# Linear attention with decay ahead of a soft mixture of experts: half of the heads with chunks of 64 tokens, scores made one chunk ahead

## The chip, the core and the metric

The kernel runs on one core of a Trainium2 chip. Five engines work side by side, each through its own list of instructions in order: TensorE (PE, with its weight loads shown apart as PEld), VectorE (DVE), ScalarE (ACT), GpSimd (POOL) and SyncE (SP), which here issues nearly all transfers. The measure is the time of one execution on the device in microseconds (us); lower is better. All data are f32.

## What is computed

The reference, cut to what matters:

```python
# B, H, S, D = 4, 8, 768, 64; block = 64
for b in range(nb):
    qb, kb, vb = q[:, :, sl], k[:, :, sl], v[:, :, sl]
    intra = einsum('bhic,bhjc->bhij', qb, kb) * Dmask      # lam**(i-j) for i >= j
    intra = einsum('bhij,bhjd->bhid', intra, vb)
    inter = einsum('bhid,bhde->bhie', qb * lam_pow, kv_state)
    out[:, :, sl] = intra + inter
    kb_dec = kb * rev_pow
    kv_state = lam_block * kv_state + einsum('bhsd,bhse->bhde', kb_dec, vb)
x = out.transpose(0, 2, 1, 3).reshape(B * S, H * D)        # 3072 x 512
logits = x @ phi                                           # 32 slots, 8 experts
d = softmax(logits, axis=0); slot_input = d.T @ x
h = relu(slot_input[e] @ w1[e]); slot_out[e] = h @ w2[e]   # for each expert e
return softmax(logits, axis=1) @ slot_out
```

The result of the attention doesn't depend on how long a block is: what lies inside a block goes through masked scores, what lies before it through the carried state.

## The kernel before

The tokens are cut into chunks of 128, 6 for each of 4 sequences, 24 in all (`T`, `NB = 6`). A head pair lies on the 128 partitions: `hh` is the half (partitions 0 to 63 or 64 to 127), `hp` one of the 4 pairs. The loop over `t` does, for every chunk:

- `scores(t)`: PE makes key times query for 8 heads into two banks (`sc`), in pieces of 64 keys, so that four instructions fill the four 64 x 64 quarters of the array. DVE multiplies them by the mask of powers of lam into `at`.
- `recall(t)`: queries decayed by POOL (`qs`, made by `decay_q`) times the state of the chunks before (`st`), into the banks `xa` and `xb`.
- `turn_k(t + 1)`: PE turns the keys of the next chunk through the bank `kv`, ACT copies them out (`kn`). For the chunks named by `loaded` a second copy of the keys, already turned, is loaded from memory instead (`kN`, 9 chunks).
- `natural(t - 1)`: PE turns the result of the last chunk (`tr`), ACT copies it to `x`.
- `attend(t)`: values times `at`, added to `xa` and `xb`; ACT copies them to `xt`.
- `state(t)`: decayed keys (`kd`, POOL) times values into `kv`; DVE adds it to the decayed state, giving `st`; POOL decays that into `dec` for the next chunk.

Every four chunks the soft mixture gets its part: in the chunk with t % 4 == 0 `logits` (bank `gl`, DVE reduction `mx`, ACT exponential `e`, DVE copy `L`), in the next one `weights` (two transposes in the bank `dp`), the first half of `slot_softmax` and `slots` (bank `gl`, DVE sum `acc`), in the third the rest of `slot_softmax` (`cs`, `CN`). After the loop come the last chunk's logits, the two layers of the experts (`first`, `second`; weights w1 in 32 slabs of 512 KB, w2) and the output (`put`: PE, a copy by ACT or DVE to `o`, a write of 256 KB `y<-o` by SP).

The order on every engine is that of the program: the class `InOrder` records each operation as it is written, so its line (L51 before, L49 after) stands for nearly all instructions, and a reader goes by the names of tiles. SP issues in program order too and waits where a buffer isn't free yet. `NLOAD` buffers take queries, keys and values; `NSLAB` slabs take weights, of which `PACE` tenths are asked for per chunk:

```python
if t + 2 < T:
    load_chunk(t + 2, (0, 1))
want = min(NSLAB, (t + 1) * PACE // 10)
load_early(want - sent)
```

PSUM, into which PE writes, has 8 banks, and all are named: sc0, sc1, xa, xb, kv, tr, gl, dp.

Of the kernel before, what the change touches and what calls it, by code (L numbers as in the profile page):

```python
# [14 lines left out]
P = 128  # L15
B, H, S, DH = 4, 8, 768, 64
# [8 lines left out]
NSLAB = 35  # L25
NLOAD = 10
# [6 lines left out]
PACE = 16  # L33


def loaded(t):

    return t == 0 or t % NB in (2, 4)
# [18 lines left out]
def decay_attn_soft_moe(  # L57
# [32 lines left out]
    def load_chunk(t, which=(0, 1, 2, 3)):  # L90
        srcs = (qT, kT, vN, kN)
        for i in which:
            if i == 3 and not loaded(t):
                continue
            tl = loads.tile([P, 512], F32, tag="ld", name="ld")
            sp.dma_start(out=tl, in_=srcs[i][t])
            IN[t, i] = tl
# [38 lines left out]
    load_chunk(0)  # L136
    load_chunk(1)
# [12 lines left out]
    wps = bank("dp")  # L150
# [15 lines left out]
    mask = work.tile([P, 2, HP, P], F32, tag="mask", name="mask")  # L166
    for hh in range(2):
        for hp in range(HP):
            x = hh * HP + hp
            dve.tensor_tensor_scan(  # L170
                out=mask[:, hh, hp, :],
                data0=lam_sb[:, x:x + 1].broadcast_to([P, P]),
                data1=ident,
                initial=0.0,
                op0=ALU.mult,
                op1=ALU.add,
            )
# [15 lines left out]
    kpow = mask.rearrange("p a b i -> p (a b) i")[:, :, P - 1:P]  # L193
# [8 lines left out]
    AT, XT, X, ST, QS, KD = {}, {}, {}, {}, {}, {}  # L202

    SC = {}

    def scores(t):
        q_, k_ = IN[t, 0], IN[t, 1]
        banks = [bank(f"sc{hh}") for hh in range(2)]

        for hp in range(HP):  # L210
            for j in range(2):
                for hh in range(2):
                    r = slice(64 * hh, 64 * hh + 64)
                    pe.matmul(
                        out=banks[hh][64 * j:64 * j + 64, hp * P:(hp + 1) * P],
                        lhsT=k_[r, hp * P + 64 * j:hp * P + 64 * j + 64],
                        rhs=q_[r, hp * P:(hp + 1) * P],
                        start=True,
                        stop=True,
                    )  # L220
        AT[t] = []
        for hh in range(2):
            at = work.tile([P, HP, P], F32, tag="at", name="at", bufs=2)
            sc = banks[hh].rearrange("p (a b) -> p a b", a=HP)
            dve.tensor_tensor(out=at, in0=sc, in1=mask[:, hh], op=ALU.mult)
            AT[t].append(at)

    def decay_q(t):
        if t < T and t % NB > 0:
            qs = work.tile([P, HP, P], F32, tag="qs", name="qs")  # L230
            pool.tensor_tensor(out=qs, in0=IN[t, 0].rearrange("p (a b) -> p a b", a=HP), in1=qpow, op=ALU.mult)
            QS[t] = qs

    def turn_k(t):

        if t < T and t % NB < NB - 1 and not loaded(t):
            tk = bank("kv")
            for hp in range(HP):
                pe.transpose(tk[:, hp * P:(hp + 1) * P], IN[t, 1][:, hp * P:(hp + 1) * P], ident)
            kn = work.tile([P, D], F32, tag="kn", name="kn")  # L240
            act.copy(out=kn, in_=tk)
            IN[t, 3] = kn

    def decay_k(t):
        if t < T and t % NB < NB - 1:
            kd = work.tile([P, H, DH], F32, tag="kd", name="kd")
            k_ = IN[t, 3]
            pool.tensor_tensor(
                out=kd.rearrange("p (a b) c -> p a b c", a=2),
                in0=k_.rearrange("p (a b c) -> p a b c" if loaded(t) else "p (b a c) -> p a b c", a=2, b=HP),  # L250
                in1=kpow.rearrange("p (a b) o -> p a b o", a=2).broadcast_to([P, 2, HP, DH]),
                op=ALU.mult,
            )
            KD[t] = kd

    XB = {}

    def place(t, hh, hp):

        g, a = divmod(hp, 2)  # L260
        return XB[t][hh][64 * a:64 * a + 64, g * P:(g + 1) * P]

    def recall(t):
        XB[t] = [bank("xa"), bank("xb")]
        if t % NB > 0:

            qs, st = QS.pop(t), ST["st"]
            for hp in range(HP):
                for hh in range(2):
                    r = slice(64 * hh, 64 * hh + 64)  # L270
                    pe.matmul(
                        out=place(t, hh, hp),
                        lhsT=st[r, hp, :],
                        rhs=qs[r, hp, :],
                        start=(hp < 2),
                        stop=True,
                        skip_group_check=True,
                    )

    def attend(t):  # L280
        n = t % NB
        v_ = IN[t, 2].rearrange("p (h c) -> p h c", h=H)
        at = AT.pop(t)
        xt = keep.tile([P, HP, P], F32, tag="xt", name="xt")
        for hh in range(2):
            for hp in range(HP):
# [3 lines left out]
                    rhs=at[hh][:, hp, :],  # L290
                    start=(n == 0 and hp < 2),
                    stop=True,
                    skip_group_check=True,
                )
            act.copy(
# [3 lines left out]

    def state(t):  # L300
        n = t % NB
        if n == NB - 1:
            return
        v_ = IN[t, 2].rearrange("p (h c) -> p h c", h=H)
        kd = KD.pop(t)
        kv = bank("kv")
        for hp in range(HP):
            for hh in range(2):
                pe.matmul(
                    out=kv[64 * hh:64 * hh + 64, hp * DH:(hp + 1) * DH],  # L310
                    lhsT=kd[:, HP * hh + hp, :],
                    rhs=v_[:, HP * hh + hp, :],
                    start=True,
                    stop=True,
                )
        kvv = kv[:, 0:HP * DH].rearrange("p (a b) -> p a b", a=HP)
        st = work.tile([P, HP, DH], F32, tag="st", name="st", bufs=2)
        if n == 0:
            dve.tensor_copy(out=st, in_=kvv)
        else:  # L320
            dve.tensor_tensor(out=st, in0=ST["dec"], in1=kvv, op=ALU.add)
        ST["st"] = st
        if n < NB - 2:
            dec = work.tile([P, HP, DH], F32, tag="dec", name="dec")
            pool.tensor_tensor(
                out=dec, in0=st, in1=lamc.broadcast_to([P, HP, DH]), op=ALU.mult
            )
            ST["dec"] = dec
# [12 lines left out]
    def logits(g):  # L341
        cs = [t for t in range(4 * g, 4 * g + 4) if t < T - 1]
        R = SL * len(cs)
        pl = bank("gl")
        for hp in range(HP):
            for c, t in enumerate(cs):
# [6 lines left out]
                )  # L353
        pl = pl[0:R, 0:P]
# [29 lines left out]
    def weights(raw=True):  # L384
        dp = bank("dp")
# [3 lines left out]
        dve.tensor_copy(out=d, in_=dp[:, 0:P])  # L389
        return dp[:, P:2 * P]  # L390

    def slot_softmax(g, lp):

        lv = lp.rearrange("p (g s) -> p g s", g=4)
# [20 lines left out]
    def slots(g):  # L415
        cs = [t for t in range(4 * g, 4 * g + 4) if t < T - 1]
        R = SL * len(cs)
        psl = bank("gl")
        for c, t in enumerate(cs):
# [6 lines left out]
            )  # L426
        if g == 0:
# [13 lines left out]
    sm = iter(())  # L441
    for t in range(T):
        if t + 2 < T:
            load_chunk(t + 2, (0, 1))

        want = min(NSLAB, (t + 1) * PACE // 10)
        load_early(want - sent)
        sent = max(sent, want)
        if t + 2 < T:
            load_chunk(t + 2, (2, 3))  # L450
# [3 lines left out]
        for _ in range((2, 4, 3)[t - T + 3] if t >= T - 3 else 0):  # L454
            load_one(*ld1)
        if t == T - 1:
            load_one(work, "kd", 1)
            load_one(work, "kn", 1)
        last = t == T - 1

        asks = t // 4 - 1 if t > 0 and t % 4 == 0 else G - 1 if last else None
        sums = t // 4 - 1 if t > 4 and t % 4 == 1 else None
        scores(t)
        if t == 0:
            decay_k(0)
            powers()
        recall(t)
        if sums is not None:
            sm = slot_softmax(sums, weights())
        if t > 0:  # L470
            turn_k(t + 1)
            if not last:
                natural(t - 1)
        if sums is not None:
            next(sm)
        if asks is not None:
            ask = logits(asks)
            next(ask)
        if last:
            next(ask)  # L480

            phi4 = [
# [312 lines left out]
```

## Time and profile before

| what | value |
|---|---|
| median of 3 runs | 169.34 us (168.54 to 169.99) |
| the profiled execution's own time | 170.31 us |
| span of the profiled execution | 168.4 us |
| mean granted clock of TensorE | 0.978 of full speed |
| busy: PE, weight loads, DVE, ACT, POOL | 149.2, 108.0, 90.7, 60.8, 64.4 us |
| matmul instructions | 2629 |
| read from and written to memory | 54.86 MB, 6.29 MB |

The span runs from the first instruction of the program to the last; the time of an execution holds some 2 us more. The rows in the next sections give the start of a group in us from the span's start, its length, engine, line, operation, the tile written <- the tiles read, shapes, the count, and in brackets the idle time ahead of it with what ended it. f32 matmuls are two instructions each, transposes one. "xa<-at,ld 128*64" is a group of matmuls on 128 rows and 64 columns of the array.

### The profile page before, as it was taken

To read this page: it belongs to the slowest core of one execution; us is meant where nothing else is said; L and a number is where in the kernel's file an instruction comes from. 1 tells how busy PE (TensorE), PEld (TensorE's weight loads), DVE (VectorE), ACT (ScalarE), POOL (GpSimd) and SP (SyncE) were. 2 spreads that over 40 slices of the span, in tenths; PEclk is the share of its full clock that TensorE was granted. 3 is DMA by queue.
4 is the path that set the end of the run, shared out by engine and by line. 5 is a ranking of instruction groups with operands and counts; after the bars stand their busy time and mean duration, and the time that the engine had idled before them with its cause. 6 is when DMAs were issued, how large, how long until landed. Compare 5 with 4: busy or idle time off the path is not lost.

```text
span 168.4 us, 6282 instructions
## 1 busy us (share of the span) xinstructions
PE 149.2 (89%) x2629; PEld 108.0 (64%) x2629; DVE 90.7 (54%) x213; ACT 60.8 (36%) x153; POOL 64.4 (38%) x86
## 2 busy tenths in 40 slices
PE   6889998997979999979999799999899999999700
PEld 6668887686867889768868677776233345546600
DVE  2665453556475647565546537575118799245800
ACT  3033442443422444342344344225010698342700
POOL 1248772245665156655252556610000295000000
PEclk9999999999999999999999999999999999999965
DMA  5999999999999999999999999899999999999795
GB/s 170 350 330 308 373 399 409 410 407 407 416 405 405 374 402 404 408 415 405 407 409 386 387 329 337 261 289 273 390 399 408 411 399 408 403 375 314 262 384 195
DMA packets 32444, 61.56 MB, mean 366 GB/s; under 512 B 3616, under 2 KB 9760, under 8 KB 32416
## 3 DMA queue, kind: packets, MB, share of 16 engines
q1 hardware_dynamic: 32272, 61.16, 97.1%
q8 instruction: 21, 0.34, 0.8%
q14 instruction: 7, 0.06, 0.1%
q10 hardware_dynamic: 144, 0.01, 0.1%
HBM read 54.86 MB, written 6.29 MB: 363 GB/s over the span
## 4 chain that ended last, share of the span: by engine, by line
PE 65%; DMA 13%; DVE 10%; issue 4%; POOL 2%; ACT 1%; DVEq 0%; POOLq 0%; ACTq 0%; SPq 0%
PE xa L51 15%; PE kv L51 13%; PE sc L51 11%; PE gl L51 8%; PE xb L51 7%; PE tr L51 7%; PE dp L51 4%; DMA slab<-w_x 4%; DMA ld<-qT 4%; DMA ld<-kT 4%; DVE at L51 2%; DVE cs L51 2%; DVE CN L51 2%; DVE o L51 1%; DMA y<-o 1%
## 5 line engine op out<-in xcount | busy, mean ns | idle before, releaser
L51 DVE TENSOR_TENSOR at<-sc,mask 128x512 f32<-128x512 f32 x48 | 30.8, 683 | 9.9 <-PE sc L51 9.9
L51 PE MATMUL sc<-ld 64*64 64x128 f32 x768 | 27.8, 282 | 0.5 <-issue 0.5
L51 POOL TENSOR_TENSOR qs<-ld,qpow 128x512 f32<-128x512 f32 x20 | 25.7, 1285 | 5.9 <-DVE qpow L51 2.9
L51 PEld LDWEIGHTS sc<-ld 64*64 64x64 f32 x768 | 21.6, 136 | 6.4 <-issue 5.3
L51 ACT COPY x<-tr 128x512 f32<-128x512 f32 x24 | 14.1, 588 | 30.1 <-PE tr L51 30.1
L51 POOL TENSOR_TENSOR dec<-st,qpow 128x256 f32<-128x256 f32 x16 | 10.0, 622 | 28.1 <-DVE st L51 28.1
L51 PE MATMUL xa<-at,ld 128*64 128x128 f32 x192 | 15.8, 285 | 3.7 <-DVE at L51 3.7
L51 DVE TENSOR_TENSOR st<-dec,kv 128x256 f32<-128x256 f32 x16 | 6.8, 422 | 20.0 <-PE kv L51 20.0
L51 POOL TENSOR_TENSOR kd<-kn,mask 128x512 f32<-128x512 f32 x11 | 11.7, 1060 | 13.0 <-ACT kn L51 13.0
L51 PEld LDWEIGHTS xa<-at,ld 128*64 128x64 f32 x192 | 10.0, 136 | 8.3 <-DVE at L51 6.1
L51 ACT COPY kn<-kv 128x512 f32<-128x512 f32 x11 | 6.4, 586 | 23.9 <-PE kv L51 19.8
L51 PE MATMUL tr<-ident,xt 128*128 128x128 f32 x96 | 15.0, 279 | 0.0
L51 PE MATMUL xb<-at,ld 128*64 128x128 f32 x192 | 14.8, 275 | 0.0
L51 PE MATMUL kv<-ld,kd 128*64 128x64 f32 x320 | 12.8, 222 | 1.2 <-ACT kn L51 0.8
L51 PE MATMUL xa<-qs,st 64*64 64x128 f32 x160 | 12.3, 270 | 1.0 <-POOL dec L51 1.0
L51 PEld LDWEIGHTS kv<-ld,kd 128*64 128x64 f32 x320 | 12.1, 138 | 1.5 <-issue 1.5
L51 PE MATMUL xb<-qs,st 64*64 64x128 f32 x160 | 12.4, 270 | 0.0
L51 PEld LDWEIGHTS tr<-ident,xt 128*128 128x128 f32 x96 | 10.8, 142 | 2.4 <-issue 2.4
L51 POOL TENSOR_TENSOR kd<-ld,mask 128x512 f32<-128x512 f32 x9 | 9.5, 1060 | 5.1 <-DVE mask L51 5.0
L51 PEld LDWEIGHTS xb<-at,ld 128*64 128x64 f32 x192 | 10.8, 136 | 0.8 <-DVE at L51 0.7
L51 ACT COPY xt<-xa 128x256 f32<-128x256 f32 x24 | 8.8, 368 | 6.4 <-PE xa L51 6.3
L51 PEld LDWEIGHTS xa<-qs,st 64*64 64x64 f32 x160 | 9.5, 133 | 1.2 <-POOL dec L51 1.2
(134 smaller groups left out, 229.2 us busy)
## 6 DMA issues: line engine op xcount, KB each, us to landing
slab<-w_x SPq DMA_DIRECT2D x32, 512.0 KB, 6.9
w2p<-w_x SPq DMA_DIRECT2D x20, 512.0 KB, 9.4
ld<-qT SPq DMA_DIRECT2D x24, 256.0 KB, 6.2
ld<-kT SPq DMA_DIRECT2D x24, 256.0 KB, 5.8
ld<-vN SPq DMA_DIRECT2D x24, 256.0 KB, 6.9
w2t<-w_x SPq DMA_DIRECT2D x24, 256.0 KB, 5.4
y<-o SPq DMA_DIRECT2D x24, 256.0 KB, 3.5
ld<-kN SPq DMA_DIRECT2D x9, 256.0 KB, 5.6
```

Source lines behind the costliest of these rows:

```text
L51: return self._tc.keep_in_program_order(f(*args, **kwargs))
```

## The change

The four pairs of heads are split: `NF = 2` pairs are fine (heads with blocks of 64 tokens, as in the reference), two are coarse (128 as before).

- Scores of a fine pair have 64 columns instead of 128, so a chunk's mask and `at` are 384 wide instead of 512 (`SCW`). `scores(t + 1)` is made in chunk t, and so is its `decay_scores`.
- `attend` is split: `attend_fine` with 64 keys and 64 queries at a time, in two calls (`cross` True and False, so that halves that run side by side write to different banks), and `attend_coarse`. After the first call ACT reads two columns of the result (`seen`), and the next writers of these banks wait for it.
- A fine pair's state moves twice in a chunk: `add_fine` makes both halves' key times value sums in the banks `ka` and `kb`, `states` (all DVE, `dec` no longer on POOL) makes `st` for the second half and `sb` for the next chunk's first half. `recall` comes last in a chunk and takes `st` of the chunk before for coarse pairs, `sb` for fine first halves and `st` of this chunk for fine second halves. Every chunk has a recall now, and a state, in the last of a sequence for the fine pairs only.
- All 24 chunks' keys are turned on the chip, two chunks ahead (`turn_k(t + 2)`, `keep_k`); `kN` is no longer loaded.
- Banks: `xa` and `xb` become one tile of two banks, `xab`; `kv` becomes `ka`, `kb` and `tk`; `gl` and `dp` are gone, and logits, weights and slots use `sc0`, that of the scores.
- Loads: keys and queries are asked for four chunks ahead, values three. w1 is loaded in two DMAs of 256 KB per slab, with 2 KB rows. `NSLAB` 33, `NLOAD` 12, `PACE` 14.

```diff
+HF = P // 2
+NF = 2
+SCW = NF * HF + (4 - NF) * P
-NSLAB = 35
-NLOAD = 10
+NSLAB = 33
+NLOAD = 12
-PACE = 16
+PACE = 14
...
+    def load_step(s):
+        load("k", s + 2)
+        load("v", s + 1)
+        load("q", s + 2)
...
-                sp.dma_start(out=t_, in_=w1[4 * Q + q, kc])
+                for i in range(2):
+                    sp.dma_start(out=t_[:, i], in_=w1[4 * Q + q, kc][:, i])
...
+    def decay_scores(t, hh):
+        if t < T:
+            dve.tensor_tensor(out=AT[t][:, hh], in0=SC[t][hh][:, 0:SCW], in1=mask[:, hh], op=ALU.mult)
...
+    def states(t):
+        st = work.tile([P, HP, DH], F32, tag="st", name="st", bufs=2)
...
+            dve.tensor_tensor(out=st[:, 0:m], in0=DEC[t - 1][:, 0:m], in1=ka[:, 0:m], op=ALU.add)
+        A[t] = st
+        yield
...
+        dve.tensor_tensor(out=dec, in0=st, in1=lamc.broadcast_to([P, HP, DH]), op=ALU.mult)
+        dve.tensor_tensor(out=sb, in0=dec[:, 0:NF], in1=kb[:, 0:NF], op=ALU.add)
+        BB[t] = sb
+        yield
+        dve.tensor_tensor(out=dec[:, 0:NF], in0=sb, in1=lamc[:, 0:NF].broadcast_to([P, NF, DH]), op=ALU.mult)
...
+    def attend_fine(t, cross):
+        if cross:
+            both = ps.tile([P, 2, 512], F32, tag="x", name="xab")
...
+        for hp in fine:
+            for j in range(2):
+                hh = 1 - j if cross else j
+                r = slice(HF * j, HF * j + HF)
+                pe.matmul(
+                    out=place(t, hh, hp, j),
+                    lhsT=v_[r, HP * hh + hp, :],
+                    rhs=AT[t][r, hh, span(hp)],
...
+        if cross:
+            act.copy(out=seen, in_=both.rearrange("p a b -> p (a b)")[:, HF:513:512 - HF])
...
     for t in range(T):
+        add_fine(t)
+        scores(t + 1)
+        if t > 0:
+            attend_fine(t, True)
+        add_coarse(t)
+        decay_k(t + 1)
+        attend_coarse(t)
+        ahead = states(t)
+        decay_scores(t + 1, 0)
+        next(ahead)
+        decay_scores(t + 1, 1)
...
+        if t > 0:
+            natural(t - 1)
+        turn_k(t + 2)
+        keep_k(t + 2)
...
+        attend_fine(t, False)
+        recall(t)
+        gather(t)
...
+        decay_q(t + 1)
```

On PE, a chunk with t % 4 == 3 before, from the turned result of the last chunk to the scores of the next (`[waits ...]` names the engine or load whose signal a row waits for):

```order
L51 MATMUL tr<-ident,xt 128x128 x4
L51 MATMUL xa<-at,ld 64x128 [waits DMAHW0_49,DVE_49]
L51 MATMUL xa<-at,ld 64x128 x3
L51 MATMUL xb<-at,ld 64x128 [waits DVE_49]
L51 MATMUL xb<-at,ld 64x128 x3
L51 MATMUL kv<-ld,kd 64x64 [waits Pool_49]
L51 MATMUL kv<-ld,kd 64x64 x7
L51 MATMUL sc_1514<-ld 64x128 [waits DMAHW2_49,DMAHW1_49,PE_49]
```

And such a chunk after the change, behind the scores of the next chunk, up to its recall (the rows with 64x64 from `at` are the fine pairs, `sb` is a fine pair's state):

```order
L49 MATMUL xab<-at,ld 64x64 [waits PE_49,Activation_49]
L49 MATMUL xab<-at,ld 64x64 x3
L49 MATMUL ka<-ld,kd 64x64 x4
L49 MATMUL xab<-at,ld 64x128 [waits Activation_49]
L49 MATMUL xab<-at,ld 64x128 x3
L49 MATMUL tr<-ident,xt 128x128 x4
L49 MATMUL tk<-ident,ld 128x128 [waits DMAHW3_49]
L49 MATMUL tk<-ident,ld 128x128 x3
L49 MATMUL xab<-at,ld 64x64 x4
L49 MATMUL xab<-qs,st 64x128 [waits Pool_49]
L49 MATMUL xab<-qs,st 64x128 x3
L49 MATMUL xab<-qs,sb 64x64 x4
```

The wait for DVE's decayed scores ahead of the values has moved away; in its place the first fine values wait for ACT's copies of the chunk before (`xt`), and the coarse values for ACT's `seen`.

On DVE, the chunk of the logits before:

```order
L51 TENSOR_REDUCE mx<-gl 128x1 [waits PE_49]
L51 SCALAR_TENSOR_TENSOR nm<-mx,nm 128x1 [waits DVE_49]
L51 TENSOR_TENSOR st<-dec,kv 128x256 [waits PE_49,Pool_49]
L51 COPY L<-gl 128x128 [waits Activation_49]
L51 SCALAR_TENSOR_TENSOR lsum<-lsum,alpha,rs 128x1 [waits Activation_49]
L51 TENSOR_TENSOR at<-sc_1971,mask 128x512 [waits PE_49]
```

And after (the bank sc_1945 holds the logits, sc_2012 the scores that PE makes next in the same place):

```order
L49 TENSOR_TENSOR dec<-st,qpow 128x256 [waits DVE_49]
L49 TENSOR_TENSOR sb<-dec,kb 128x128 [waits DVE_49]
L49 TENSOR_REDUCE mx<-sc_1945 128x1 [waits PE_49]
L49 SCALAR_TENSOR_TENSOR nm<-mx,nm 128x1 [waits DVE_49]
L49 COPY L<-sc_1945 128x128 [waits Activation_49]
L49 SCALAR_TENSOR_TENSOR lsum<-lsum,alpha,rs 128x1 [waits Activation_49]
L49 TENSOR_TENSOR dec<-sb,qpow 128x128
L49 TENSOR_TENSOR at<-sc_2012,mask 128x384 [waits PE_49]
```

The logits' readers (`mx`, ACT's `e`, then `L`) now stand ahead of the next scores in one bank, and the decays of the state have come from POOL to DVE.

More of the change, by code (lines that the diff above doesn't have):

```diff
@@ L298, in attend @@
         XT[t] = xt
[L300 to L328, printed above, removed]
     def natural(t):
@@ L426, in slots @@
             )
+        yield
         if g == 0:
@@ L451, in decay_attn_soft_moe @@
         if t == 0:
             load_phi()
-        for _ in range((2, 4, 3)[t - T + 3] if t >= T - 3 else 0):
+        for _ in range((8, 3)[t - T + 2] if t >= T - 2 else 0):
             load_one(*ld1)
[L456 to L463, printed above, removed]
-        if t == 0:
-            decay_k(0)
-            powers()
@@ L467, in decay_attn_soft_moe @@
-        recall(t)
[L468 to L478, printed above, removed]
-        if last:
-            next(ask)
-            phi4 = [
-                work.tile([P, 2, 4, SL], F32, tag=tg, name="phi4", bufs=n) for tg, n in (("dec", 1), ("st", 2))
-            ]
-            for i in range(2):
-                two = phi_sb[:, 2 * i:2 * i + 2].rearrange("p (a o) s -> p a o s", o=1)
-                pool.tensor_copy(out=phi4[i], in_=two.broadcast_to([P, 2, 4, SL]))
@@ L488, in decay_attn_soft_moe @@
-        attend(t)
-        if last:
-            weights(raw=False)
-            cm = bank("kv")
-            pe.matmul(out=cm[:, 0:4], lhsT=blk_, rhs=gm, start=True, stop=True)
-            dve.tensor_reduce(out=own, in_=cm[:, 0:4], axis=AX.X, op=ALU.min)
+        turn = t // 4 - 1 if t > 3 else None
+        if t == 0:
+            attend_fine(0, True)
+            turn_k(1)
+            keep_k(1)
+        add_fine(t)
+        scores(t + 1)
+        if t > 0:
+            attend_fine(t, True)
@@ new lines, in decay_attn_soft_moe @@
+        add_coarse(t)
[5 more added lines that the diff above has]
+        decay_scores(t + 1, 1)
+        for _ in range(1):
+            next(ahead, None)
+        phase = t % 4 if turn is not None else 3
+        if phase == 1:
+            dp = weights()
+        if t > 0:
+            natural(t - 1)
+        turn_k(t + 2)
+        keep_k(t + 2)
+        if last or phase == 0:
+            ask = logits(G - 1 if last else turn)
+            next(ask)
+            for _ in ask:
+                pass
+        elif phase == 1:
+            dve.tensor_copy(out=d, in_=dp[:, 0:P])
+            sm = slot_softmax(turn, dp)
+            next(sm)
+        elif phase == 2:
+            for _ in slots(turn):
+                pass
+            for _ in sm:
+                pass
@@ L500, in decay_attn_soft_moe @@
             dve.tensor_reduce(out=gsel, in_=ident.rearrange("p (g s) -> p g s", g=4), axis=AX.X, op=ALU.add)
-        decay_q(t + 1)
-        state(t)
-        decay_k(t + 1)
-        if asks is not None and not last:
-            next(ask)
-        if sums is not None:
-            slots(sums)
-        elif t % 4 == 2:
-            for _ in sm:
-                pass
         if t == 1:
             pool.tensor_copy(out=blk, in_=sel.rearrange("p (o s) -> p o s", o=1).broadcast_to([P, 4, SL]))
-    natural(T - 2)
+    phi4 = [
+        work.tile([P, 2, 4, SL], F32, tag=tg, name="phi4", bufs=n) for tg, n in (("dec", 1), ("st", 2))
+    ]
+    for i in range(2):
+        two = phi_sb[:, 2 * i:2 * i + 2].rearrange("p (a o) s -> p a o s", o=1)
+        pool.tensor_copy(out=phi4[i], in_=two.broadcast_to([P, 2, 4, SL]))
+    dp = weights(raw=False)
+    dve.tensor_copy(out=d, in_=dp[:, 0:P])
+    cm = bank("ka")
+    pe.matmul(out=cm[:, 0:4], lhsT=blk_, rhs=gm, start=True, stop=True)
+    dve.tensor_reduce(out=own, in_=cm[:, 0:4], axis=AX.X, op=ALU.min)
     load_one(*ld1)
-    for _ in range(2):
-        load_one(work, "at", 2)
-    load_one(work, "qs", 1)
+    for tg, n in (("kd", 1), ("kn", 1), ("at", 2), ("mask", 1), ("at", 2), ("qs", 1), ("qpow", 1)):
+        load_one(work, tg, n)
     negm = run["m"]
```

304 lines of the change are left out of this document (190 added, 114 removed).

## The prediction

> **What bounds the kernel now.** I read the busy time by stretch first, then PE's order of time inside a chunk, then the chain of waits. The columns of the first fence are start and end of a stretch in us, its length, the busy time of PE, weight load, DVE, ACT and POOL with instruction counts, granted clock, DMA share, GB/s.
>
> ```profile
> 11.56:109.84 98.28, 92.90 (x2005) 76.43 (x2002) 54.00 (x118) 35.93 (x95) 53.50 (x55) 1.00 1.01 383
> 118.66:145.83 27.17, 27.17 (x298) 10.40 (x299) 15.96 (x40) 12.33 (x31) 7.11 (x20) 1.00 1.05 404
> 145.83:156.80 10.97, 10.91 (x103) 6.67 (x103) 5.76 (x10) 4.42 (x8) 0.00 (x0) 1.00 0.93 330
> 156.80:168.40 11.60, 1.92 (x14) 1.59 (x12) 2.92 (x5) 2.27 (x5) 0.00 (x0) 0.68 0.84 296
> ```
>
> The 22 chunks from the second to the last but one take 98.28 us. PE is busy for 92.90 of them and DMA is full as well, so the next question is which of the two waits. A chunk in order of time (start, length, what; xN counts instructions, and each f32 matmul is two of them) answers it:
>
> ```profile
> 52.38 1.10 PE L51 MATMUL sc<-ld 64*64 64x128 f32 x32
> ...
> 53.31 0.27 PE L51 MATMUL xa<-qs,st 64*64 64x128 f32 x1
> 53.31 0.27 PE L51 MATMUL xb<-qs,st 64*64 64x128 f32 x1
> 53.32 0.27 PE L51 MATMUL xa<-qs,st 64*64 64x128 f32 x1
> 53.33 0.27 PE L51 MATMUL xb<-qs,st 64*64 64x128 f32 x1
> 53.42 0.27 PE L51 MATMUL xa<-qs,st 64*64 64x128 f32 x1
> ...
> 53.86 0.66 PE L51 MATMUL tr<-ident,xt 128*128 128x128 f32 x4
> 54.44 0.66 PE L51 MATMUL xa<-at,ld 128*64 128x128 f32 x8
> 54.93 0.61 PE L51 MATMUL xb<-at,ld 128*64 128x128 f32 x8
> 55.37 0.63 PE L51 MATMUL kv<-ld,kd 128*64 128x64 f32 x16
> 55.93 1.10 PE L51 MATMUL sc<-ld 64*64 64x128 f32 x32
> ...
> 57.41 0.66 PE L51 MATMUL kv<-ident,ld 128*128 128x128 f32 x4
> 57.90 0.60 PE L51 MATMUL tr<-ident,xt 128*128 128x128 f32 x4
> ```
>
> PE works in rounds. Four 64*64 instructions start within 0.02 us (53.31 to 53.33) and the next four 0.11 later (53.42), so a round of 128 columns costs 0.11. The kv row, 16 instructions of 64 columns, two at a time, gives (0.63 - 0.22) / 7 = 0.058 for a round of 64 columns, where 0.22 is one instruction's length. This chunk takes 55.93 - 52.38 = 3.55 with no wait in it. A turn of the keys (57.41 to 57.90, and one change of shape shared with tr) adds 0.44. So the stage is PE's own work, plus these waits:
>
> ```profile
> 34.25 0.63 PE L51 MATMUL kv<-ident,ld 128*128 128x128 f32 x4 [0.29 <-DMA ld<-kT]
> 39.80 0.66 PE L51 MATMUL xa<-at,ld 128*64 128x128 f32 x8 [0.94 <-DVE at L51]
> 75.88 0.66 PE L51 MATMUL xa<-at,ld 128*64 128x128 f32 x8 [1.00 <-DVE at L51]
> 93.88 0.66 PE L51 MATMUL xa<-at,ld 128*64 128x128 f32 x8 [0.93 <-DVE at L51]
> ...
> 28.31 0.76 PE L51 MATMUL sc<-ld 64*64 64x128 f32 x18 [0.46 <-issue]
> 84.34 0.55 PE L51 MATMUL kv<-ident,ld 128*128 128x128 f32 x3 [0.23 <-issue]
> 104.68 0.51 PE L51 MATMUL kv<-ld,kd 128*64 128x64 f32 x11 [0.41 <-issue]
> ...
> 45.02 2.07 issue
> ```
>
> PE waits 0.29 us for a load in the whole stage: DMA is full because it is fed ahead, not because it is late. DVE's decayed scores (at) cost 2.9 us in three places; waits for nothing that the profile shows cost 1.1 here, and some 1.1 more in the chunk of the last row, where POOL stood for 2.07. Behind the stage, PE is busy for all of 118.66 to 145.83, and the last stretches are output writes.
>
> **Work on PE, over 22 chunks.** Scores: half of the 8 rounds shrink from 128 to 64 columns, 4 x 0.051 = 0.20 per chunk, -4.5 us. Values (attend): 8 rounds of 0.11 with 128 rows become 4 of these and 4 rounds of four 64*64 instructions with 64 columns, again -0.20, -4.5. Recall: 4 rounds of 0.11 become 2 and 4 small ones, equal; three first chunks of a sequence now recall too (0.12), three last ones now make a state (0.23): +1.1. State: 8 rounds of 0.058 stay 8. Keys are turned in 21 of these chunks instead of 10: 11 x 0.44 = +4.8. Changes of tile shape stay three in a chunk. Sum -3.1.
>
> The small round, four 64*64 instructions with 64 columns, does not occur in the trace. Below it is bounded by 0.058 / 2 shared among more rows (0.03), above by the sc round (0.11); I take 0.058, since kv shows a weight load and a matmul of 64 columns turning round in that time, and the rows at 53.31 show four issued in 0.02. At 0.11 all 16 small rounds of a chunk cost 0.05 more, 17.9 us in 22 chunks. The Trainium skill ("TensorE: Matmul & The Clock Gate", Part 1) speaks for that side: it gives a start to start that never drops below about 25 ns however few columns there are, which would make a round of four 0.100 and add 14.8 us. The trace has starts of 0.01 apart inside a round of four, so I do not follow it.
>
> **Waits that go.** Scores made a chunk ahead leave a whole chunk to DVE: -2.9. Late next is nothing on DVE: two at of 384 columns (0.55 each, from the rows below), st 0.42, and dec, sb, dec, some 0.9, are 2.4 of a chunk of 3.7; in the chunk with the slot softmax it runs 0.3 into the next one, where it has slack. POOL loses dec and gains kd in four chunks, and ends each a microsecond before its use. ACT gains kn in 13 chunks and is full only between the turn and xt.
>
> ```profile
> L51 DVE TENSOR_TENSOR at<-sc,mask 128x512 f32<-128x512 f32 x48 | 30.8, 683 | 9.9 <-PE sc L51 9.9
> L51 DVE TENSOR_TENSOR st<-dec,kv 128x256 f32<-128x256 f32 x16 | 6.8, 422 | 20.0 <-PE kv L51 20.0
> L51 DVE SCALAR_TENSOR_TENSOR acc<-acc,alpha,gl 128x512 f32<-128x512 f32 x4 | 3.0, 747 | 3.7 <-PE gl L51 3.7
> L51 ACT ACTIVATION_READ_ACCUMULATOR e<-gl,nm 128x1 f32 x5 | 1.0, 193 | 0.0
> ...
> 61.51 1.08 PE L51 MATMUL gl<-xt,phi_sb 128*32 128x128 f32 x32
> 62.66 0.29 DVE L51 TENSOR_REDUCE mx<-gl 128x1 f32<-128x128 f32 x1 [0.76 <-PE gl L51]
> 62.98 0.16 DVE L51 SCALAR_TENSOR_TENSOR nm<-mx,nm 128x1 f32<-128x1 f32 x1
> 63.24 0.37 ACT L51 ACTIVATE e<-gl,nm 128x128 f32<-128x128 f32 x1 [0.62 <-PE xa L51]
> 64.47 0.28 DVE L51 COPY L<-gl 128x128 f32<-128x128 f32 x1
> ```
>
> **Waits that come.** (1) seen: after the first fine values PE must wait until ACT has copied two columns; everything of the chunk stands behind it. 0.22 for the matmul, 0.04 to ACT, some 0.19 for the copy (the read row is the nearest), 0.05 back make 0.50 from the last matmul's start; change of shape and the coarse state cover 0.43, and the first round after a wait starts some 0.03 late, its weights not yet loaded. I take 0.10 a chunk, +2.2; at least 0, and 0.3 (+6.6) where ACT is still in the xt copies. (2) The logits, the weights and the slot sums now use the bank of the scores, so the next scores wait for their readers. Logits: from the end of gl (62.59) to the end of e is 1.02, and L follows e: 0.28 and 0.1, so the bank is free 1.6 after the last logit starts, where PE has 1.05 of other work (change of shape 0.2, fine values 0.17, recall 0.45, fine state 0.23): 0.55 x 5 = 2.8. Slots, read by acc in 0.75, and weights come out at 0.12 each by the same count: 1.2. Together +4.0; at least 0 (DVE and ACT faster than here), at most 6.5.
>
> **Start, end, output.**
>
> ```profile
> 5.59 1.94 PE L51 MATMUL sc<-ld 64*64 64x128 f32 x32
> ...
> 11.56 1.10 PE L51 MATMUL sc<-ld 64*64 64x128 f32 x32
> ...
> 109.84 1.10 PE L51 MATMUL sc<-ld 64*64 64x128 f32 x32
> ...
> 114.47 1.06 PE L51 MATMUL sc<-xt,phi 128*128 128x128 f32 x8
> ```
>
> The first scores run at half pace, 1.94 / 8 or some 0.21 a round. After the change PE has ahead of its second chunk: from 5.59 a turn of keys (1.0, to 6.6), scores (1.3, to 7.9), the wait for two at (to 9.0), first values and a turn (to 9.9), fine state and the next scores (to 10.8), coarse state and values (to 11.7), another turn and the recall (to 12.65). That is 1.1 after 11.56. In the last chunk the logits end 3.5 after its start, and mx, nm and e (1.0) and two xt copies (0.9) stand in one line behind them: the last logits of all come 5.5 after the chunk's start, where it was 114.47 - 109.84 = 4.63: +0.9. Unexplained waits and the DMA wait, 2.5 in all: per chunk DMA now moves 3 loads and 1.4 slabs, 1.52 MB or 3.75 us at 404 GB/s, against 4.4 us of PE, so it is no longer full; PE fetches a quarter more instructions. I take -1.8, between 0 and -2.5.
>
> ```profile
> ld<-qT SPq DMA_DIRECT2D x24, 256.0 KB, 6.2
> ...
> ld<-kN SPq DMA_DIRECT2D x9, 256.0 KB, 5.6
> ...
> 145.83 18.68 SPq L51 DMA_DIRECT2D y<-o x24
> ```
>
> Nine kN loads, 2.36 MB or 5.8 us of DMA, fall away, but hidden behind PE they bring nothing in the stage; nor do the split rows of w1 cost there (32 more issues on SP, which has 0.64 us for each). They count at the end: outputs start at 145.83 with loads still ahead of them, and the last 11.60 us are writes. With the loads in earlier: -1.2 (0 to -2.7).
>
> **Sum.** -3.1 - 2.9 + 2.2 + 4.0 + 1.1 + 0.9 - 1.8 - 1.2 = -0.8, on a span of 168.4: 167.6. The profiled execution took 170.31, 1.9 over its span and 0.97 over the median of 169.34, so the median to expect is about 168.5.
>
> **Rivals.** Faster: seen and the shared bank cost nothing, because PE's waits fall into time that it loses anyway, the unexplained waits go and the end gives its 2.7: -2.2 - 4.0 - 0.7 - 1.5 = -8.4 against my sum, 160; half of it, 164, is likelier. For it: ACT and DVE have idle time in every chunk. Against: both waits stand in the program order with nothing between. Slower by the waits: at their upper ends, with no relief of the unexplained ones, +4.4 + 2.5 + 1.8 = +8.7, some 177; with half of it 173. From 0.21 a chunk on seen alone makes it over 1%. For it: ACT has x, kn, e and xt in one line ahead of the next seen. Slower by the small rounds: at 0.11 it is 168.5 + 17.9 = 186; against it stand the rows at 53.31. (By the floor that the Trainium skill's page states it would be 183.) The change that does not bring its saving: eight DMAs of 256 KB in flight instead of mixed ones run dry while SP waits for a buffer, and loads come late; with the 0.3 of the row at 34.25 in half of the chunks, 172. Against: a load is asked for two and a half chunks or 9 us ahead of its use and takes 6.2.
>
> **Chances.** Within 1% (what a measurement of this kernel can just tell from no change): 0.36. Faster 0.34. Slower 0.30: waits 0.20, small rounds 0.07, loads 0.03. The likeliest is no change, at 168.5. From 161 to 176 leaves out the small rounds and the edges of the two others, under 0.2.
>
> **What would show it.** Right: sc rows of 32 at about 0.9 us, fine groups of 8 at 0.06 a round, plain chunks of 3.6 to 3.7, no DVE at ahead of PE, DMA under full before 100 us, PE at xab waiting for seen by 0.1. Wrong: a chunk of 4.2 or more with seen, or DVE L and acc ahead of sc, as the cause; fine groups at 0.1 a round; PE waiting for ld.

## The result, and the profile after

The changed kernel takes 185.11 us (median of 4 runs, 183.82 to 185.94) where the kernel before takes 168.94 (168.22 to 169.99) beside it: 1.0939 times as long, with a 95% interval of 1.0879 to 1.0999. The forecast was no change, 168.5, with a range of 161 to 176. The profiled execution has a span of 184.2, which is 15.8 more than before. Each later run was measured beside the kernel before anew (medians of 169.06 to 169.46); executions over 1.5% slower than the fastest of their kernel count in the medians given, but not in the ratios.

The first lines of the page of the changed kernel, with the granted clock and the DMA share in 40 slices:

```profile
PE 157.2 (85%) x3257; PEld 111.8 (61%) x3257; DVE 112.1 (61%) x282; ACT 70.1 (38%) x190; POOL 61.3 (33%) x78
PEclk9999999969999999999999999879999999999965
DMA  5995899998899889989989989984899999999995
```

PE is busy for 8 us more than before (149.2), with a quarter more instructions (3257 against 2629 matmuls). The other half of the loss is time in which it stands still. The clock dips twice, near 39 and 120 us, besides the end. By stretch (same columns as in the prediction):

```profile
9.35:116.96 107.61, 96.97 (x2555) 78.45 (x2547) 73.59 (x182) 44.15 (x128) 48.97 (x46) 0.98 0.93 318
36.25:42.50 6.25, 6.04 (x120) 4.44 (x111) 3.03 (x7) 1.56 (x5) 1.78 (x3) 0.73 0.95 328
116.96:128.23 11.27, 9.90 (x189) 6.51 (x190) 6.64 (x19) 3.18 (x11) 3.10 (x4) 0.85 0.72 242
128.23:148.12 19.89, 18.31 (x170) 6.57 (x174) 8.96 (x29) 4.94 (x15) 1.15 (x5) 1.00 0.99 358
```

The first row runs from the scores of the second chunk to those of the last (98.28 before). The last logits start at 128.23 instead of 114.47, so 13.8 of the 15.8 are lost in the attention. Transfers are not the bound there: they fell from 383 to 318 GB/s. A plain chunk that nothing disturbs:

```profile
20.29 0.85 PE L49 MATMUL sc<-ld 64*64 64x64 f32 x32
21.00 0.34 PE L49 MATMUL xab<-at,ld 64*64 64x64 f32 x8
21.27 0.45 PE L49 MATMUL ka<-ld,kd 128*64 128x64 f32 x8
21.68 0.66 PE L49 MATMUL xab<-at,ld 128*64 128x128 f32 x8
22.27 0.66 PE L49 MATMUL tr<-ident,xt 128*128 128x128 f32 x4
22.77 0.60 PE L49 MATMUL tk<-ident,ld 128*128 128x128 f32 x4
23.30 0.34 PE L49 MATMUL xab<-at,ld 64*64 64x64 f32 x8
23.46 0.40 PE L49 MATMUL xab<-qs,st 64*64 64x128 f32 x8
23.68 0.29 PE L49 MATMUL xab<-qs,sb 64*64 64x64 f32 x8
23.80 0.30 PE L49 MATMUL xab<-qs,st 64*64 64x64 f32 x8
...
24.15 0.24 PE L49 MATMUL sc<-ld 64*64 64x64 f32 x4
```

It takes 24.15 - 20.29 = 3.86, where 3.7 was forecast. Two chunks that are disturbed show what the forecast did not have (in order of time on PE; idle time and what ended it in brackets):

```profile
33.44 0.29 PE L49 MATMUL xab<-qs,st 64*64 64x64 f32 x6
35.87 0.27 PE L49 MATMUL xab<-qs,st 64*64 64x64 f32 x2 [2.14 <-issue]
...
36.25 1.30 PE L49 MATMUL sc<-ld 64*64 64x64 f32 x32
37.25 0.51 PE L49 MATMUL xab<-at,ld 64*64 64x64 f32 x8
37.69 0.69 PE L49 MATMUL ka<-ld,kd 128*64 128x64 f32 x8
38.17 1.12 PE L49 MATMUL xab<-at,ld 128*64 128x128 f32 x8
39.22 1.00 PE L49 MATMUL tr<-ident,xt 128*128 128x128 f32 x4
...
56.41 0.45 PE L49 MATMUL sc<-ld 64*64 64x64 f32 x13
57.54 0.67 PE L49 MATMUL sc<-ld 64*64 64x64 f32 x18 [0.69 <-issue]
```

At 33.5 PE stops after 6 of 8 equal recall instructions, and at 56.6 after 13 of 32 score instructions. Nothing that the program orders can end there, since the instructions of a group wait for nothing between them. Behind the first of these gaps the same rows take up to twice as long (1.12 instead of 0.66, 1.00 instead of 0.66), at a granted clock of 0.73 in the mean of this stretch: it was 0.50 from 36.56 to 39.97.

Counting the instructions of PE and PEld in the trace from the first (semaphore instructions too), these gaps stand at equal distances, and each ends soon after a packet of 16 KB of the queue that the page calls q8 instruction ("had stood" is the time from the start of the instruction ahead of the gap):

```
kernel   instruction no.  PE goes on at  had stood  last 16 KB packet starts  from there
before    961 = 193+3*256      28.31       0.72          26.13                  2.18
before   1729 = 193+6*256      48.49       1.22          46.18                  2.31
before   3265 = 193+12*256     84.34       0.51          81.96                  2.38
before   3777 = 193+14*256     98.62       0.44          96.37                  2.25
before   4033 = 193+15*256    104.68       0.68         102.06                  2.62
after    1473 = 193+5*256      35.87       2.36          33.34                  2.53
after    2497 = 193+9*256      57.54       0.91          54.99                  2.55
after    3265 = 193+12*256     73.82       0.78          71.35                  2.47
after    5057 = 193+19*256    110.81       1.09         108.38                  2.43
after    5313 = 193+20*256    116.84       1.81         114.45                  2.39
```

The queue also moves about one of these packets per 256 instructions of PE: 21 for a list of 5354 instructions before, 26 for 6606 after, 27 for 6890 in b_sc64 below (20.9, 25.8 and 26.9 times 256); in the other runs the two agree within one. That is theory F, late code: PE's list is fetched in pieces of 16 KB, 256 instructions; a piece is fetched after the one ahead of it has been entered; and in these ten rows it can be used some 2.4 us after its packet starts. Between the entry and the packet lie 0.2 to 5.1 us (middle value 3.5 before, 2.1 after), a time in which the data transfers fill the DMA engines. A border is late when the instructions of a piece last less than that delay plus 2.4. Before, a piece lasts 6.1 us in the middle, after the change 5.3, gaps included. The rival, theory W, is that the change lost its time in waits for engines (seen, the shared bank, DVE's state) and that instructions cost nothing beyond their work. In the expectations, "before" and "b_" stand for the kernel before, "a_" for the changed one.

### The profile page after: what moved, and what is told of

Its sections match the earlier page's. It is cut to its first block, busy times and chain, and to the rows that moved or that the text cites. A ratio compares the mean times of both kernels' runs of the same rounds, so it can differ in the third digit from the quotient of the medians.

```text
span 184.2 us, 7698 instructions
## 1 busy us (share of the span) xinstructions
PE 157.2 (85%) x3257; PEld 111.8 (61%) x3257; DVE 112.1 (61%) x282; ACT 70.1 (38%) x190; POOL 61.3 (33%) x78
## 4 chain that ended last, share of the span: by engine, by line
PE 68%; DMA 10%; DVE 7%; issue 6%; SPq 1%; ACT 1%; DVEq 0%; ACTq 0%
PE xab L49 21%; PE sc L49 17%; PE ka L49 11%; PE tr L49 9%; PE tk L49 6%; DMA w2t<-w_x 6%; DMA y<-o 5%; PE kb L49 4%; DVE at L49 1%; SPq L49 1%; DVE acc L49 1%; DVE dec L49 1%; DVE cs L49 1%; DVE o L49 1%; DVE h L49 0%
## 5 line engine op out<-in xcount | busy, mean ns | idle before, releaser
L49 POOL TENSOR_TENSOR qs<-ld,qpow 128x512 f32<-128x512 f32 (+1 forms) x24 | 27.4, 1142 | 47.9 <-issue 46.4
L49 DVE TENSOR_TENSOR at<-sc,mask 128x384 f32<-128x384 f32 x48 | 26.4, 552 | 21.9 <-PE sc L49 21.8
L49 PE MATMUL xab<-at,ld 64*64 64x64 f32 (+1 forms) x576 | 33.8, 258 | 3.5 <-ACT seen L49 1.3
L49 POOL TENSOR_TENSOR kd<-kn,kpow 128x512 f32<-128x512 f32 x24 | 25.2, 1051 | 22.4 <-PE ka L49 14.7
L49 PEld LDWEIGHTS xab<-at,ld 64*64 64x64 f32 (+1 forms) x576 | 22.3, 136 | 15.7 <-issue 8.3
L49 PE MATMUL sc<-ld 64*64 64x64 f32 (+1 forms) x768 | 22.4, 250 | 3.5 <-issue 2.2
L49 PE MATMUL ka<-ld,kd 64*64 64x64 f32 (+1 forms) x352 | 20.2, 229 | 0.9 <-issue 0.9
L49 ACT COPY xt<-xab 128x256 f32<-128x256 f32 x48 | 15.5, 377 | 3.5 <-PE xab L49 2.8
L49 PEld LDWEIGHTS ka<-ld,kd 64*64 64x64 f32 (+1 forms) x352 | 15.0, 137 | 1.7 <-issue 0.3
L49 PE MATMUL tk<-ident,ld 128*128 128x128 f32 x96 | 14.7, 276 | 0.0
```

The lines of the kernel that those rows point to most:

```text
L49: return self._tc.keep_in_program_order(f(*args, **kwargs))
```

## The experiments

### More instructions, same work (b_sc64)

```diff
-                        out=banks[hh][64 * j:64 * j + 64, hp * P:(hp + 1) * P],
+                        out=banks[hh][64 * j:64 * j + 64, hp * P + 64 * i:hp * P + 64 * i + 64],
-                        rhs=q_[r, hp * P:(hp + 1) * P],
+                        rhs=q_[r, hp * P + 64 * i:hp * P + 64 * i + 64],
```

> The kernel before with the same scores in pieces of 64 columns: 64 matmuls and 64 weight loads a chunk instead of 32 and 32, same multiplications. Theory F (code fetch): PE's list comes in pieces of 256 instructions (16 KB); in both traces PE stands still in the middle of a group only at such a border, some 2.4 us after the fetch starts, and the fetch starts 0.2 to 5 us (3.3 in the middle) after the piece before was entered. A piece now lasts about 4.2 us of work instead of 5.8, so most borders are late: 10 to 30 us longer, 180 to 200, with gaps inside groups at equal distances of 256. Theory W (waits for engines made the change slow, the number of instructions costs nothing): 16 rounds of 0.058 instead of 8 of 0.11 are 0.05 a chunk, so 169 to 171.

187.11 us in one run, 18 more than the kernel before (169.06). An undisturbed score group takes 0.98 instead of 0.92 (75.61 to 76.59 below), so the work itself grew by 1.3 in 22 chunks. Of 22 borders ahead of the last logits 14 are late, by 19.3 us from start to start of instructions (before 5 of 16, by 3.6; after the change 5 of 21, by 6.9). The waits of PE (sum in us, times, longest), and two late borders in order of time:

```profile
PE sc L51 <- issue: 10.9, 11, 1.9
PE kv L51 <- issue: 2.5, 1, 2.5
...
14.49 0.28 PE L51 MATMUL kv<-ld,kd 128*64 128x64 f32 x2
17.30 1.01 PE L51 MATMUL kv<-ld,kd 128*64 128x64 f32 x14 [2.54 <-issue]
...
56.56 1.10 PE L51 MATMUL sc<-ld 64*64 64x64 f32 x61 [1.84 <-issue]
...
75.61 1.16 PE L51 MATMUL sc<-ld 64*64 64x64 f32 x64
76.59 0.27 PE L51 MATMUL xa<-qs,st 64*64 64x128 f32 x1
```

This is the kernel before, without seen, shared banks or fine pairs, and it loses as much as the change did. W falls as the only cause.

### The same with fewer transfers at a time (b_sc64_p6, a_p6)

```diff
-PACE = 16
+PACE = 6
-        want = min(NSLAB, (t + 1) * PACE // 10)
+        want = min(NSLAB, (t + 1) * PACE // 10 if t < T - 2 else NSLAB)
```

> As b_sc64, with 6 tenths of a weight slab asked for per chunk instead of 16, the rest at the end. F, with the fetch waiting behind data: a chunk now moves 1.1 MB, the fetch starts within 1.5 us, and most of b_sc64's gaps go: the last logits of all end within 4 us of those of the kernel before (114.5). The whole takes longer at the end, where weights come late. If the fetch doesn't wait for data: gaps as in b_sc64. W: no gaps in either.

198.5 us in one run, late at the end as expected. The last logits start at 123.99 instead of 132.16, with 9 late borders and 11.3 us of gaps instead of 14 and 19.3; the packet starts 2.0 after the entry (middle value) instead of 3.2. So two fifths of the gaps go with the transfers, not most of them as expected, and the last logits come 9.5 later than in the kernel before, where 4 was expected: 254 to 260 GB/s still flow in this stage, and a piece of 256 instructions is short.

In the changed kernel the edit is `PACE = 6` instead of 14:

> The changed kernel with 6 tenths of a slab per chunk instead of 14, the rest of the weights at the end. F: the gaps at the borders of 256 instructions go, and the half-clock stretches behind the two long ones: the last logits start 7 to 10 us earlier than 128.2, at 118 to 121, while the end is late for weights (time unknown, 180 to 200). W: the bank waits, seen and DVE don't hang on the loads: last logits at 127 to 128.

197.66 us in one run. The last logits start at 122.37, 5.9 earlier than with 14; W said 0 to 1, F 7 to 10. Both missed: the gaps did not go as F expected. The list of PE is the same, instruction for instruction, and five of its borders are still late, by 0.5, 0.6, 0.4, 1.2 and 1.3, together 4.0 from start to start instead of 6.9. The packet starts 2.0 after the entry in the middle, hardly less than the 2.1 with 14. The other 3.0 of the gain is the clock, which stays full in the stage: the chunk that took 6.25 behind the long gap takes 4.85 (34.62 to 39.47):

```profile
9.00:112.67 103.67, 95.68 (x2554) 77.25 (x2547) 72.67 (x182) 44.26 (x128) 48.84 (x46) 1.00 0.81 254
...
34.24 0.27 PE L49 MATMUL xab<-qs,st 64*64 64x64 f32 x2 [0.22 <-issue]
...
34.62 0.88 PE L49 MATMUL sc<-ld 64*64 64x64 f32 x32
...
35.94 0.66 PE L49 MATMUL xab<-at,ld 128*64 128x128 f32 x8
36.54 0.66 PE L49 MATMUL tr<-ident,xt 128*128 128x128 f32 x4
...
39.47 0.34 PE L49 MATMUL sc<-ld 64*64 64x64 f32 x8 [0.21 <-DVE acc L49]
...
54.53 0.67 PE L49 MATMUL sc<-ld 64*64 64x64 f32 x18 [0.96 <-issue]
```

### Fewer instructions, same products (b_sc128)

```diff
-            for j in range(2):
-                for hh in range(2):
-                    r = slice(64 * hh, 64 * hh + 64)
-                    pe.matmul(
-                        out=banks[hh][64 * j:64 * j + 64, hp * P:(hp + 1) * P],
-                        lhsT=k_[r, hp * P + 64 * j:hp * P + 64 * j + 64],
+            for hh in range(2):
+                r = slice(64 * hh, 64 * hh + 64)
+                pe.matmul(
+                    out=banks[hh][:, hp * P:(hp + 1) * P],
+                    lhsT=k_[r, hp * P:(hp + 1) * P],
```

> The kernel before with scores of 64 rows and 128 columns of the array: 16 matmuls of 128 columns a chunk, two at a time, instead of 32 of 64 by 64, four at a time. The same 8 rounds of 0.11, with a third fewer instructions in the piece (144 instead of 176 a chunk). F: a piece lasts 7 us, longer than any delay seen but one, so the gaps inside groups (0.7, 1.1, 0.4, 0.2, 0.4, some 3 in all) go: 166 to 167. W: no change, 168 to 170. If two halves of the rows that use the same columns don't run side by side, scores take twice as long: 185 or more.

170.15 us, ratio 1.0037 (0.9998 to 1.0076). By its time W is nearest; the trace says otherwise. A piece lasts 7.4 us, none of 13 borders is late, and the waits of PE have no row with issue at all:

```profile
PE xa L51 <- DVE at L51: 3.0, 4, 0.8
PE dp L51 <- DVE warm L51: 1.5, 1, 1.5
PE kv L51 <- ACT kn L51: 0.8, 1, 0.8
PE kv L51 <- DMA ld<-kT: 0.5, 1, 0.5
...
51.92 1.16 PE L51 MATMUL sc<-ld 64*128 64x128 f32 x16
53.01 0.32 PE L51 MATMUL xa<-qs,st 64*64 64x128 f32 x1
```

What the 3 us of gaps gave went into the scores: 53.01 - 51.92 = 1.09 instead of 0.92, and a change of shape ahead of the recall (0.60 instead of 0.55 for its group), 0.22 a chunk or 4.8 in 22. PE's waits for DVE's at fell from 3.7 to 3.0, and the stage came out at 98.54 instead of 98.28. My expectation had taken the round as equal.

### The shared bank (a_tr, a_nf0, a_nf0_tr)

```diff
-        pl = bank("tk" if g == G - 1 else "sc0")
+        pl = bank("tk" if g == G - 1 else "tr")
```

> The changed kernel with the logits in the bank of the turned results (tr) instead of that of the scores. If the waits ahead of the scores in five chunks (0.3, 0.75, 1.1, 0.74 and part of 1.0 us, which end 0.1 after DVE's copy L) are the shared bank's: 3 us saved, less some 0.1 a time for the copy of the turned result, and F gives part of it back: 181.5 to 183.5. If they are late code (the profile puts them down to issue): 184.5 to 185.5.

183.54 us, ratio 1.0798 (1.0700 to 1.0895) against 1.0939 (1.0879 to 1.0999): 1.5 less, at the upper end of what was expected, but the intervals overlap, so the time alone shows no gain. The last logits start 3.75 earlier (124.48); 3.0 of that is the half-speed clock, which this execution didn't have, so little is left for the bank. The row that the profile put down to issue was the bank's: an undisturbed chunk with logits falls from 5.62 (86.52 to 92.14) to 5.06 (84.07 to 89.13 in a_tr). In the changed kernel, DVE's copy and then the scores:

```profile
71.48 0.29 DVE L49 COPY L<-sc 128x128 f32<-128x128 f32 x1 [0.58 <-ACT e L49]
...
71.87 0.57 PE L49 MATMUL sc<-ld 64*64 64x64 f32 x20 [0.91 <-issue]
```

Part of it came back as other waits in a_tr: 1.2 for ACT's copy x (0.24 a time), and 1.4 instead of 0.5 for ACT's xt, which stands behind e in ACT's list.

With no fine pair (all four coarse, so that `attend_fine`, `seen` and the second state step fall away) what is left of the change is scores a chunk ahead, turned keys, shared banks and split rows:

```diff
-NF = 2
+NF = 0
-NSLAB = 33
+NSLAB = 32
```

> The changed kernel with no fine pair (all heads carry their state by 128): scores a chunk ahead, keys turned on the chip (but for the last chunk of a sequence), shared banks, 2 KB rows stay; fine values, seen and the second state step are gone, and NSLAB is 32 for space. 88 matmuls a chunk instead of 112. F: few gaps at the borders, the work is that of before plus ten turns (4.9) less the waits for decayed scores (2.9) plus the shared bank (some 4): 172 to 176. W: PE has 9 us more work in scores and values than the changed kernel and saves 3.4 of seen, 2.2 of slower fine values and 1 of DVE: 185 to 189.

179.06 us, ratio 1.0613 (1.0558 to 1.0668), between the two. W falls: a plain chunk takes 4.09 of PE instead of 3.86, and the time is 6 us shorter. A piece of code lasts 6.4 us in the middle instead of 5.3, and one border is late, by 0.6 (at 21.59), instead of five by 6.9. But the larger part of the loss is there without any fine pair. F had the price of the shared bank too low. Its two rows among the waits of PE (the first is the scores behind the logits, put down to the recall ahead of them):

```profile
PE sc L49 <- PE xab L49: 3.7, 4, 0.9
PE sc L49 <- DVE acc L49: 2.3, 4, 0.9
```

With a fifth of the first kind this is some 7 us. In the changed kernel the same waits are shorter (5.7, below), because fine values and states stand between.

> The same move of the logits in the kernel without fine pairs, where no gap falls on a border of 256 instructions in these chunks and each takes 6.16 us, 1.06 more than its work. Shared bank: 5 times 0.9 to 1.06 saved, 174 to 175. If the wait has another cause: 179.

177.45 us, ratio 1.0453 (1.0369 to 1.0538). Four of the five chunks fell from 6.16 to 5.36 and one, with a late border in it, to 5.78, which is 3.6 in all, but the last logits came only 0.9 earlier (121.33 instead of 122.27): the next chunk waits for ACT's xt (1.6 in four places), two borders became late (0.5 each on PE's idle time), and the first scores start 0.5 later. A wait that was removed was paid for again at the next engine in line.

### seen, and the rows of 2 KB (a_seen, a_rows)

```diff
-        attend_coarse(t)
         ahead = states(t)
...
         turn_k(t + 2)
         keep_k(t + 2)
+        attend_coarse(t)
```

> The changed kernel with the coarse values (the row behind seen) moved behind the turns of the result and of the keys, so that 1.0 us of PE work covers ACT's copy. The trace shows 0.12 of wait in a plain chunk (0.40 instead of 0.28 for the coarse state) and 0.38 in the last chunk of a sequence; one more change of shape costs 0.05 to 0.1 a chunk. If seen is a small term: 0.5 to 2 us saved, 183 to 184.6. If seen is what makes the change slow: 5 us or more saved, under 180.

185.23 us, ratio 1.0875 (1.0783 to 1.0967): the interval overlaps that of the changed kernel, so no difference is shown; 5 us, or 3%, would be. In the trace a plain chunk takes 3.84 instead of 3.86 and the last one of a sequence 3.73 instead of 3.95. seen is a small term.

```diff
-                for i in range(2):
-                    sp.dma_start(out=t_[:, i], in_=w1[4 * Q + q, kc][:, i])
+                sp.dma_start(out=t_, in_=w1[4 * Q + q, kc])
```

> The changed kernel with w1 loaded as before, one transfer of 512 KB with rows of 4 KB per slab instead of two of 256 KB with rows of 2 KB. F: the fetch waits for the bytes that are queued ahead of it, which stay the same: no change, 184 to 186. If smaller rows make loads or the code fetch late: 181 to 183. If they help: 187 or more.

184.97 us, ratio 1.0915 (1.0826 to 1.1005). The rows of 2 KB cost or bring nothing that can be measured (the interval is some 1.5 us wide to either side); the packet with code starts 2.2 after the entry, as with them (2.1).

### What remains of the gain in the kernel before (b_sm, b_sm_p14, b_sm_turn)

```diff
         recall(t)
+        if t % 4 == 2:
+            for _ in sm:
+                pass
...
-        elif t % 4 == 2:
-            for _ in sm:
-                pass
```

> The kernel before with the second half of the slot softmax (cs, CN on DVE, 1.8 us) recorded right behind the decayed scores of its chunk instead of behind the state, so that it no longer stands ahead of the next chunk's decayed scores. The three waits of PE for DVE (0.94, 1.00, 0.93) go. If they are worth what they show: 169.0 - 2.9 = 166.1. F: freed PE reaches the borders of its pieces earlier and gives up to a third back: 166 to 167.

167.53 us, ratio 0.9899 (0.9823 to 0.9975): faster than both kernels, by 1% instead of the 1.7% of the waits. The three waits for at are gone (cs and CN now end at 72.0, ahead of the scores of 72.47), and late borders took a part back: 7 with 4.8 us instead of 5 with 3.6. On DVE, in order of time:

```profile
71.74 0.29 DVE L51 TENSOR_TENSOR CN<-ce,cs 128x128 f32<-128x128 f32 x1
72.65 0.42 DVE L51 TENSOR_TENSOR st<-dec,kv 128x256 f32<-128x256 f32 x1 [0.62 <-PE kv L51]
73.62 1.29 DVE L51 TENSOR_TENSOR at<-sc,mask 128x512 f32<-128x512 f32 x2 [0.55 <-PE sc L51]
```

The next edit changes `PACE` from 16 to 14 in this kernel:

> b_sm (the kernel before with the slot softmax recorded earlier) with 14 tenths of a slab per chunk instead of 16. F: fewer bytes ahead of each fetch, which starts some 0.4 earlier; of b_sm's gaps at borders (0.5, 0.4, 1.5, 0.8, 0.45, 0.5, 0.3, some 4.5 in all) about a third goes: 166 to 167, if the later weights don't delay the end. If the end is set by the transfers: 167.5 to 169.

Its four runs lie between 166.99 and 172.09 (median 170.22), too far apart for a ratio. The profiled execution (169.72) doesn't bear F's expectation out: the packet starts 3.4 after the entry in the middle, as in b_sm, and 5 late borders cost 6.6 instead of a third less than 4.8. What the time would be stays open.

The last one turns all keys on the chip in b_sm (`loaded(t)` is true for the first chunk alone):

> b_sm with all keys turned on the chip (but for the first chunk): eight loads of 256 KB less, eight turns more, 0.43 each, which is 3.4 us of PE. F: the stage moves 2.1 MB less, so fetches start some 0.5 earlier and 1 to 2 us of gaps go: 168.5 to 170. If turned keys cost only their work: 170.5 to 171.5. If the end is set by the transfers: 167 or less.

168.2 us, ratio 0.9973 (0.9929 to 1.0018), 0.7 over b_sm (1.2 by the ratios, whose intervals overlap) and a little below the expected 168.5 to 170. Eight turns are 3.4 us of PE, and late borders fell from 7 with 4.8 us to 3 with 2.2: in these two traces most of the price of turned keys came back as shorter gaps, with the packet 2.9 after the entry instead of 3.4.

## Why the prediction was wrong

The forecast added up to -0.8 on the span; it became +15.8, a miss of 16.6. By its own steps:

- **Unexplained waits: the step that failed.** It says of them and the DMA wait "2.5 in all", notes that "PE fetches a quarter more instructions", and takes "-1.8, between 0 and -2.5". The right quantity was named and then left out: the range had no positive end. Late borders cost 2.4 + 0.9 + 0.6 + 0.3 + 1.8 = 6.0 after the change, where what seen and the bank would have cost at 73.82 and 110.81 is left out. The half-speed stretches behind the two long gaps cost 3.0 more: 1.4 in the chunk from 36.25 (6.25 against 4.85 in a_p6), and 1.6 from 116.96 to the recall's end (5.71 against 4.14 in a_p6). Before, late borders and the DMA wait were 3.5 (1.0 more than the forecast had read from the idle times; the 1.1 that it saw beside POOL's row at 45.02 was the late border at 48.49). The step was +5.5, a miss of 7.3: 1.8 that was to go and didn't, 2.5 of later code, 3.0 of clock. That late code is the cause of the gaps is shown by b_sc64, where more instructions for the same products made them, and b_sc128, where fewer ended them. The 3.0 need not come in every execution: in the profiled ones of a_tr, a_seen and a_rows the clock stays full in the stage, with late borders of 6.5, 6.7 and 7.8 from start to start (6.9 here).
- **Work on PE.** The small round is right: `sc` 0.71 for 4 rounds of 0.11 and 4 of 0.058, recall 0.45, fine states 0.23, turns 0.43. The fine values are not: 8 instructions take 0.16 (23.30 to 23.46), 0.05 more than two rounds of 0.058, where eight of the recall take 0.11 to 0.12 (23.68 to 23.80). Twice a chunk this is +2.3, so the -3.1 of the forecast was some -0.8. Why these rounds are slower was not tried.
- **Waits that go.** Right: -2.9; only the first chunk still waits for at, and that wait stood in the forecast of the start. But "late next is nothing on DVE" failed once: at 86.34 PE waits 0.9 for DVE's sb, and the recall ahead of it loses 0.2: +1.1.
- **seen.** 0.12 in 19 chunks (0.40 instead of 0.28 for the coarse state) and 0.38 in the four without a coarse state, 3.8 instead of 2.2 and inside its bounds. The forecast had priced only chunks with coarse state ahead of the wait.
- **Shared bank.** The right mechanism, sized a little low: 0.5, 0.75, 1.1, 0.9 and 0.75 behind the logits, 1.2 behind the slots, and 0.1 each for the first scores after such waits, 5.7 instead of 4.0 (bound 6.5). a_tr and a_nf0_tr show that it is the bank.
- **Start.** The forecast let the first scores run at half pace (1.94 / 8 is 0.24 and not 0.21); they took 0.90 from 6.18, at full pace. The second chunk starts at 11.87 where 12.65 was forecast, and stops at once for DVE's sb, to 12.44: -0.3 in all.
- **Outputs.** -1.2 was forecast and +2.0 came. The forecast had loads done earlier because nine are left out; but 318 instead of 383 GB/s flowed in the stage, and as much was left to move behind the last logits as before (53.93 us at 356 GB/s before, 55.97 at 353 after, 19.2 and 19.8 MB). Whether PE's waits or the lower `PACE` held the transfers back was not tried. Of the +2.0, 0.7 is a wait of PE for DVE's h; the rest was not taken apart.

7.3 + 2.3 + 1.1 + 1.6 + 1.7 - 0.3 + 3.2 = 16.9 for a miss of 16.6. Of the rivals, "slower by the waits" had 173 to 177: seen came at 3.8 where it had up to 6.6, the bank at 5.7 where it had up to 6.5. That is 3.3 over the forecast, and with the 1.8 of relief that didn't come it explains some 5 us of the 16.6. "Slower by the small rounds" had 186, near the time, but its mechanism did not occur: rounds of four 64 by 64 instructions take 0.058. What was to show the forecast wrong did not list the cause: it looked for longer rounds, seen, L or acc, or ld ahead of a chunk, and not for gaps inside a group, of which the profile before had four (the fifth late border stood ahead of the recall at 48.49 and was put down to POOL's dec, which had ended 0.7 earlier).

On late code, the Trainium skill ("Runtime: NRT & Kernel Launch", section on instruction fetch mechanics) says that an engine's instructions are refilled in blocks of 16 KiB, 256 instructions, the next one while the current one executes, and that crossing a border is "mostly hidden". The runs agree with the size (gaps at distances of 256) and with the fetch one block ahead; they disagree on the cost, which was some 3 us before, 6 after and 19 in b_sc64.

## What to carry to other kernels

Gaps inside a group of equal instructions that the profile puts down to issue are a budget of their own: count the instructions from gap to gap, look for the code packet ahead of each, and compare how long 256 instructions last with the delay of the packet plus 2.4 us. A change that cuts work into more, smaller instructions beside a full DMA must pay for that, even if every round is as short as hoped; where the same products can be had with fewer instructions, the gaps go (b_sc128), though something else may take the time; thinner transfers took away only two fifths of them (19.3 to 11.3 in b_sc64_p6, 6.9 to 4.0 in a_p6). And a wait that goes is rarely worth its length: b_sm kept some 1.9 of 2.9, a_nf0_tr 1.6 of 3.6.

## What was not expected of the hardware

- The code for PE can come late beside full transfers: from entering a piece to the packet with the next one 0.2 to 5.1 us pass in the two kernels, in the middle 3.5 at 383 GB/s before and 2.1 at 318 after. With fewer transfers it fell from 3.2 (330 GB/s) to 2.0 (260) in b_sc64, but hardly in the changed kernel (2.0 at 254), so the rate alone doesn't set it; what else does wasn't found. A late piece starts to run 2.2 to 2.6 us after its packet starts in the two kernels; elsewhere some took longer, up to 4.5 (the gap that ends at 17.30 in b_sc64).
- Idle gaps of 2.1 and 1.6 us were followed by 3.4 us at a granted clock of 0.50 each (36.56 to 39.97 and 118.48 to 121.89), which cost 1.4 and 1.6; so was one of 2.5 in b_sc64 (17.34 to 20.74). Not each such gap does it: behind those of 1.84 at 56.56 in b_sc64 and 2.15 at 115.60 in a_rows the clock is 1.00. What decides it was not found.
- Two row halves that use the same 128 columns of the array run side by side (64x128 in b_sc128), but a round takes some 0.02 longer than with four quarters: 1.09 against 0.92 for 8 rounds.
